# A seven-product mixer kernel: factors and sums of weights issued by ScalarE, stores held back, the last batch's loads begun earlier

## The chip, the cores and the metric

The kernel runs on one core of one Trainium2 chip. The metric is the device time of one execution in microseconds (us); the median of several runs counts, and lower is better.

## What is computed

Four batches of chunked attention (8 heads, 768 positions, head size 64), each followed by a mixer over positions (rank 32) and one over channels (512 to 2048 to 512).

```python
for c in range(nc):                                  # 24 chunks of 32 queries
    k_full = np.concatenate([mem_k, k[:, :, l_start:r_end]], axis=2)
    v_full = np.concatenate([mem_v, v[:, :, l_start:r_end]], axis=2)
    scores = scale * np.matmul(q_c, k_full.transpose(0, 1, 3, 2))
    a = np.exp(scores - np.max(scores, axis=-1, keepdims=True))
    a = a / (np.sum(a, axis=-1, keepdims=True) + 1e-09)
    out[:, :, c_start:c_end] = np.matmul(a, v_full)
...
h = x.transpose(0, 2, 1) @ U @ V                     # x: the attention, heads side by side
u = x + h.transpose(0, 2, 1)
return u + np.maximum(u @ w_ch1, 0.0) @ w_ch2
```

## The kernel before, in words

A batch has six tiles of 128 positions, `x`, in two blocks of three. The wide layer has 16 slices `f` of 128. One w1 step makes `ph` = W1[f] times u of a block in a bank of `ps_h`; ScalarE writes its Relu rounded (`hh`), VectorE the remainder (`hl`); one w2 step (`w2_step`) is nine matmuls of 512 columns that add hh x w2 high, hh x w2 low and hl x w2 high to three banks. `hh` and `hl` come from the pool `hid`, three buffers of each.

Batches 0 and 1 run this plainly (`both_blocks`, `ffn`). During batch 1, `mix` (GpSimd) and `sums` (VectorE subtracts and adds, ScalarE rounds) make, for each of the eight pairs p of slices, five sums and two copies of weights and store them in DRAM (`s_d`): the factors. Each is 256 KB.

Batches 2 and 3 run `fast`: for each p, `products(p)` does seven products in place of eight (`PRODUCTS`; six matmuls of 384 columns each, in three banks b1, b2, b3) and combines them (`ta`, `tb`) into two hidden slices of block 0, whose `hh`, `hl` are made at once (`hid_`), and two of block 1, which are kept in float (`kept`). `first_block(p)` runs the two w2 steps of block 0, as a rule behind `products(p + 1)`; `second_block` makes hh and hl of eight kept slices and runs their w2 steps, once half way and once at the end. A factor's buffer is single: `fetch_factor` can load the factor of p + 1 only when the product of p that reads it has run. The fold of the next batch (`fold_both`: transposes, sums and roundings for `th`, `tl`) is laid between the w2 steps of a batch's last `second_block`.

The attention of batch b + 1 is a generator whose pieces (turn keys, turn queries, scores, softmax, weights times values, the rank-32 mixer) are called between the steps of batch b: `place(n)` runs n pieces. In `fast`, `fast_border` is called after the third and the seventh product, after each w2 step of `first_block` and after those of the first `second_block`; `PLACES` lists the borders at which a piece stands. Its loads are another generator; `serve(n)` issues n of them.

The order on TensorE (PE) and GpSimd is that of the code, written by hand, and so is that of SyncE's queue (SP), which issues every DMA of these batches. SP works strictly in order: a DMA that has to wait holds all behind it. VectorE and ScalarE are ordered by a scheduler from priorities. Buffers of the pool `tk` (19 slots) serve x, loads of k and q, sums, and more; a slot is free again when its last reader, a store too, has ended.

```python
    def fast_border():
        serve(2)
        place(PLACES.count(passed[0]))
        passed[0] += 1
...
                if p + 1 < NF // 2:
                    fetch_factor(p + 1, n)
                elif not last:
                    fetch_factor(0, n)
```

Of the kernel before, what the change touches and what calls it, by code (L numbers as in the profile page):

```python
# [50 lines left out]
SUMS = (("s1", 0, 0, 1, 1, "add"), ("s2", 1, 0, 1, 1, "add"), ("s5", 0, 0, 0, 1, "add"),  # L51
        ("s6", 1, 0, 0, 0, "subtract"), ("s7", 0, 1, 1, 1, "subtract"))
PRODUCTS = (("s5", 6, 0), ("a22", 2, 1), ("s1", 0, 2), ("a11", 1, 0), ("s2", 5, 1), ("s7", 4, 2), ("s6", 3, 0))
PLACES = [0, 2, 4, 6, 8, 10, 11, 13, 14, 16, 18, 20, 22, 23, 24, 25, 27, 29, 31, 33, 35]


@with_exitstack
def chunk_attn_then_mixer_kernel(
# [1035 lines left out]

    x_d = {(b, t): dram.tile([P, CH], F32, name=f"xd{b}_{t}") for b in range(1, B) for t in range(NT)}

    def put_by(b, t):
        nc.sync.dma_start(out=x_d[b, t], in_=xs.pop((b, t)))

    def recall(b, blk):  # L1100
        for t in range(blk * TB, blk * TB + TB):
# [40 lines left out]
    def add_to_x(b, t, bank, last):  # L1142
        x = xs[(b, t)]
        nc.vector.tensor_tensor(out=x, in0=bank, in1=x, op=ALU.add)
        if last:
            nc.sync.dma_start(out=out[b, t * P:(t + 1) * P, :], in_=xs.pop((b, t)))

    accs = {}

# [43 lines left out]
    def both_blocks(pieces, following):  # L1193

        units = []
        for f in range(SPLIT + LEAD):
            if f < SPLIT:
                units.append((0, f, 0, f == 0, None))
            if f >= LEAD:
                g = f - LEAD  # L1200
                units.append((1, g, 1, g == 0, False if g == SPLIT - 1 else None))
        units += [(0, f, 0, False, True if f == NF - 1 else None) for f in range(SPLIT, NF)]
        units += [(1, f, 0, f == SPLIT, True if f == NF - 1 else None) for f in range(SPLIT, NF)]
        prev = []
        for n, (blk, f, where, begins, ends) in enumerate(units):
            while done[0] < min(2 * NF, 2 * f + 1 + (n > LATE)):
                advance(1)
                more_w()
            if n == 2:
                head.close()  # L1210
            solo = n >= 2 * SPLIT
            if n == 2 * SPLIT:
                paced.close()
            for blk_, m, *_ in units[n:n + AHEAD + 1]:
                if m >= SPLIT and blk_ == 1:
                    get_w1l(m)
            if n + AHEAD >= len(units):
                get_w1l(n + AHEAD - len(units))
            w1l = w1ls[f]
            if f >= SPLIT or blk == 1:  # L1220
                del w1ls[f]
            if n == 2 * SPLIT - SOON:
                place(1)
            serve(RATEL if n < 2 * SPLIT else RATES)
            if n > 2 * SPLIT:
                border()
            if n == 0:
                for c, g3 in rest[:2]:
                    join_uT1(turn_x1(c), c, g3)
            hid_ = w1_step(0, blk, f, w1l)  # L1230
            if n == 0:
                decode(2, 4)
                for c, g3 in rest[2:]:
                    join_uT1(turn_x1(c), c, g3)
                decode(1, 1)
                decode(2, 6)
                decode(1, 6)
                decode(3, 2)
            for _ in range(RATE + (3 < n < 12)):
                advance(1)  # L1240
                more_w()
            if n > 2 * SPLIT:
                border()
            prev.append((blk, f, where, begins, ends) + hid_)
            if solo or n % 2 == 0 or ends:
                while len(prev) > (not ends):
                    while done[0] < 2 * prev[0][1] + 2:
                        advance(1)
                        more_w()
                    if n == len(units) - 1 and len(prev) == 1:  # L1250
                        place(TB)
                    w2_step(0, *prev.pop(0))
        following()
# [32 lines left out]
    def store_sums():  # L1286
        while unstored:
            to, s = unstored.pop(0)
            nc.sync.dma_start(out=to.bitcast(F32), in_=s.bitcast(F32))

    def sums(n):
        store_sums()
        for p, name, fa, ca, fb, cb, op in todo[:n]:
            s = slot([P, NCK, P], F32R, "s")
            hi, lo = s[:, 0:2, :], s[:, 2:4, :]
            a, b_ = (whole[2 * p + f][:, 2 * c:2 * c + 2, :] for f, c in ((fa, ca), (fb, cb)))
            nc.vector.tensor_tensor(out=lo.bitcast(F32), in0=a, in1=b_, op=getattr(ALU, op))
            nc.scalar.copy(out=hi, in_=lo.bitcast(F32))
            nc.vector.tensor_tensor(out=lo, in0=lo.bitcast(F32), in1=hi.bitcast(F32), op=ALU.subtract)
            unstored.append((s_d[p, name], s))  # L1300
        del todo[:n]

    def ffn(b, blk, pieces, following):
        prev = []
        for f in range(NF):
            m = f + AHEAD
            if m < NF:
                get_w1l(m)
            elif following is not None:
                get_w1l(m - NF)  # L1310
            serve(RATEL)
            if f % 2 == 0:
                place(pieces[f])
            w1l = w1ls.pop(f)
            hid_ = w1_step(b, blk, f, w1l)
            if b + 1 == CLASSIC and blk == NBLK - 1 and f == NF - 1:
                open_fast()
                for n in range(len(PRODUCTS)):
                    fetch_factor(0, n)
            sums(3)  # L1320
            if f // 2 in MIX[blk]:
                mix(f, w1l)
            if f == NF - TB:
                recall(b, blk)
            if f % 2 == 1:
                place(pieces[f])
            if blk == NBLK - 1 and f == NEARLY:
                open_turned()
            if f >= NF - TB - blk and following is not None:
                following()  # L1330
            prev.append((f, 0, f == 0, True if f == NF - 1 else None) + hid_)
            if f % 2 == 1:
                while len(prev) > (f < NF - 1):
                    w2_step(b, blk, *prev.pop(0))
# [51 lines left out]
    passed = [0]  # L1386

    def fast_border():
        serve(2)
        place(PLACES.count(passed[0]))  # L1390
        passed[0] += 1

    factors = {}

    def fetch_factor(p, n):
        name = PRODUCTS[n][0]
        if n < WLO:
            s = wlo.tile([P, NCK, P], F32R, name="w1l")
        else:
            s = fast_pools[0].tile([P, NCK, P], F32R, name="s", bufs=len(PRODUCTS) - WLO)  # L1400
        nc.sync.dma_start(out=s.bitcast(F32), in_=s_d[p, name].bitcast(F32))
        factors[p, n] = s

    def split_hidden(src):
# [8 lines left out]
    def seven(b, kept, last):  # L1413
# [5 lines left out]
        def products(p):  # L1419
# [8 lines left out]
            for n, (name, i, at_) in enumerate(PRODUCTS):  # L1428
                s = factors.pop((p, n))
                parts = [(s, c, t, c) for c in range(2) for t in (th, tl)] + [(s, 2 + c, th, c) for c in range(2)]  # L1430
                for m, (w, wc, t, c) in enumerate(parts):
# [1 line left out]
                        out=banks[at_], lhsT=w[:, wc, :], rhs=t[:, i, c, :], start=(n < 3 and m == 0),  # L1433
                        stop=(m + 1 == len(parts)), skip_group_check=True,
                    )
                if p + 1 < NF // 2:
                    fetch_factor(p + 1, n)
                elif not last:
                    fetch_factor(0, n)
                with tc.high_priority(offset=HIGH):  # L1440
                    if n == 0:
                        nc.scalar.copy(out=ta, in_=b1)
                    elif n == 1:
                        nc.vector.tensor_tensor(out=ta, in0=b2, in1=ta, op=ALU.subtract)
                    elif n == 2:
                        nc.vector.tensor_tensor(out=tb, in0=b3, in1=ta, op=ALU.add)
                    elif n == 3:
                        nc.scalar.copy(out=kept[2 * p], in_=b1)
                    elif n == 4:
                        hid_[1] = split_hidden(b2)  # L1450
                        nc.vector.tensor_tensor(out=tb, in0=tb, in1=b2, op=ALU.subtract)
                    elif n == 5:
                        nc.vector.tensor_tensor(out=ta, in0=b3, in1=ta, op=ALU.add)  # L1453
                    else:
                        nc.vector.tensor_tensor(out=kept[2 * p + 1], in0=b1, in1=tb, op=ALU.add)
                        hid_[0] = split_hidden(ta)
                if n in (2, 6):
                    fast_border()
            made[p] = hid_
# [17 lines left out]
    def fast(b, following):  # L1477
        n = NF // 2
        products, first_block, second_block = seven(b, {}, b == B - 1)
        passed[0] = 0  # L1480
        for p in range(n):
            if p == n // 2:
                first_block(p - 1)
            products(p)
            if p not in (0, n // 2):
                first_block(p - 1)
            if p == n // 2 - 1:
                recall(b, 1)
                second_block(list(range(n)), False, fast_border)
        recall(b, 0)  # L1490
        second_block(list(range(n, NF)), True, following)
        first_block(n - 1)

    manual = ExitStack()
    manual.enter_context(tc.manual_schedule(engines=FRONT))
# [83 lines left out]
```

## Time and profile before

| what | us |
|---|---|
| median of 3 runs | 688.99 (683.79 to 690.68) |
| profiled execution, its time | 686.5 |
| profiled execution, its span | 684.4 |
| TensorE busy in the span | 647.9 |
| VectorE busy | 359.4 |
| ScalarE busy | 248.6 |
| batch 2 (`fast`) begins, ends | about 375, 551 |
| batch 3 ends | 684 |

A row of waits names the engine and line that stood, what it stood for, the total, the number of times and the longest. A row of windows gives each engine's busy time in that stretch, then the clock that TensorE was granted (1.00 is 2.4 GHz, 0.50 is 1.2 GHz), the mean busy share of the 16 DMA engines and what they moved. In a timeline, brackets hold the idle time ahead of an instruction and what ended it. PE is TensorE, DVE VectorE, ACT ScalarE, SPq the issuing queue of SyncE. Line numbers (L1401) are those of the kernel before.

### The profile page before, as it was taken

To read this page: it belongs to the slowest core of one execution; us is meant where nothing else is said; L and a number is where in the kernel's file an instruction comes from. 1 tells how busy PE (TensorE), PEld (TensorE's weight loads), DVE (VectorE), ACT (ScalarE), POOL (GpSimd) and SP (SyncE) were. 2 spreads that over 40 slices of the span, in tenths; PEclk is the share of its full clock that TensorE was granted. 3 is DMA by queue.
4 is the path that set the end of the run, shared out by engine and by line. 5 is a ranking of instruction groups with operands and counts; after the bars stand their busy time and mean duration, and the time that the engine had idled before them with its cause. 6 is when DMAs were issued, how large, how long until landed. Compare 5 with 4: busy or idle time off the path is not lost.

```text
span 684.4 us, 15529 instructions
## 1 busy us (share of the span) xinstructions
PE 647.9 (95%) x6246; PEld 561.8 (82%) x6246; DVE 359.4 (53%) x735; ACT 248.6 (36%) x616; POOL 45.8 (7%) x72
## 2 busy tenths in 40 slices
PE   7798999999999999889999779899899999999997
PEld 6577999998879998778898668778788799879975
DVE  5977988676535254684537224255434943323323
ACT  4656776565223334342224222332122611212120
POOL 3700000000002122103000000000000000000000
PEclk9999999999999999999999998999999999999999
DMA  8897672583517959695573755941546175507502
GB/s 206 193 326 257 202 242 68 152 232 90 163 49 230 253 153 278 220 296 181 170 256 132 236 149 127 249 101 52 157 140 189 57 245 172 153 1 206 163 1 92
DMA packets 145760, 116.98 MB, mean 171 GB/s; under 512 B 89882, under 2 KB 109082, under 8 KB 145690
## 3 DMA queue, kind: packets, MB, share of 16 engines
q1 hardware_dynamic: 145594, 115.87, 56.9%
q8 instruction: 49, 0.80, 0.5%
q0 software_dynamic: 96, 0.13, 0.1%
q14 instruction: 21, 0.17, 0.1%
HBM read 85.16 MB, written 29.88 MB: 168 GB/s over the span
## 4 chain that ended last, share of the span: by engine, by line
PE 83%; DMA 6%; SPq 4%; DVE 3%; ACT 2%; issue 1%; POOL 0%; ACTq 0%; DVEq 0%
PE ps_h L1130 18%; PE acc L1179 16%; PE ps_h L1432 12%; PE acc L1184 8%; PE ps_a L1432 5%; PE ps_h L1179 4%; PE ps_a L1179 4%; PE ps_a L582 2%; PE ps_a L1184 2%; DMA kn<-in_k_dram 2%; PE ps_a L759 2%; PE ps_h L1184 2%; PE ps_a L656 2%; DMA vb<-in_v_dram 1%; DMA xd<-x 1%
## 5 line engine op out<-in xcount | busy, mean ns | idle before, releaser
L1179 PE MATMUL acc<-w,hh 128*128 128x512 f32 x438 | 114.5, 396 | 1.0 <-DVE w L367 1.0
L1179 PEld LDWEIGHTS acc<-w,hh 128*128 128x128 f32 x438 | 80.2, 188 | 18.9 <-issue 2.5
L1130 PE MATMUL ps_h<-ul,w1h 128*128 128x384 f32 x252 | 85.2, 342 | 2.9 <-issue 2.9
L1130 PE MATMUL ps_h<-uh,w1h 128*128 128x384 f32 x252 | 87.8, 351 | 0.0
L1137 DVE SCALAR_TENSOR_TENSOR hl<-ps_h,hh 128x384 fp32r<-128x384 f32 x63 | 35.0, 555 | 71.4 <-ACT hh L1136 71.0
L1136 ACT ACTIVATE hh<-ps_h 128x384 fp32r<-128x384 f32 x63 | 30.9, 493 | 105.7 <-PE ps_h L1130 105.6
L1184 PE MATMUL acc<-w,hl 128*128 128x512 f32 x219 | 61.8, 390 | 0.0
L1432 PE MATMUL ps_h<-th,w1l 128*128 128x384 f32 x192 | 58.5, 356 | 0.0
L1130 PE MATMUL ps_h<-uh,w1l 128*128 128x384 f32 x252 | 54.7, 339 | 0.0
L1130 PEld LDWEIGHTS ps_h<-uh,w1h 128*128 128x128 f32 x252 | 48.4, 192 | 5.6 <-issue 3.6
L1130 PEld LDWEIGHTS ps_h<-ul,w1h 128*128 128x128 f32 x252 | 48.3, 192 | 1.5 <-issue 0.5
L1184 PEld LDWEIGHTS acc<-w,hl 128*128 128x128 f32 x219 | 41.1, 188 | 8.8
L1130 PEld LDWEIGHTS ps_h<-uh,w1l 128*128 128x128 f32 x252 | 45.3, 189 | 0.0
L1408 DVE SCALAR_TENSOR_TENSOR hl<-kept,hh 128x384 fp32r<-128x384 f32 x32 | 17.9, 558 | 45.0 <-PE ps_a L1184 39.1
L1432 PEld LDWEIGHTS ps_h<-th,w1l 128*128 128x128 f32 x192 | 36.9, 197 | 1.9 <-DVE part L1453 1.0
L1432 PE MATMUL ps_h<-th,s 128*128 128x384 f32 x128 | 35.7, 339 | 0.0
L1179 PE MATMUL ps_a<-w,hh 128*128 128x512 f32 x118 | 33.5, 396 | 1.8 <-ACT hh L1136 1.8
L1408 DVE SCALAR_TENSOR_TENSOR hl<-ps_a,hh 128x384 fp32r<-128x384 f32 x16 | 8.9, 559 | 48.9 <-ACT hh L1407 48.9
L1407 ACT ACTIVATE hh<-kept 128x384 fp32r<-128x384 f32 x32 | 16.8, 525 | 47.4 <-PE ps_a L1179 41.1
L1432 PE MATMUL ps_h<-tl,w1l 128*128 128x384 f32 x96 | 33.4, 348 | 0.0
L1179 PE MATMUL ps_h<-w,hh 128*128 128x512 f32 x104 | 31.9, 429 | 0.0
L1277 POOL TENSOR_TENSOR wv<-w1h,w1l 128x512 f32<-128x512 f32 x16 | 21.2, 1325 | 125.4 <-DMA w1l<-w1ld 114.1
(274 smaller groups left out, 1150.4 us busy)
## 6 DMA issues: line engine op xcount, KB each, us to landing
w1l<-w1ld SPq DMA_DIRECT2D x39, 256.0 KB
rw<-in_moe_w_ch_dram SPq DMA_DIRECT2D x14, 512.0 KB
out_dram<-x SPq DMA_DIRECT2D x24, 256.0 KB
vb<-in_v_dram SPq DMA_DIRECT2D x56, 98.0 KB
raw<-in_moe_w_ch_dram SPq DMA_DIRECT2D x20, 256.0 KB
qn<-in_q_dram SPq DMA_DIRECT2D x36, 128.0 KB
xd<-x SPq DMA_DIRECT2D x18, 256.0 KB
x<-xd SPq DMA_DIRECT2D x18, 256.0 KB
```

Of the source, the lines that this page charges most:

```text
L582: nc.tensor.transpose(out=psv[:, p, r, :], in_=half[:, r, 2 * p:2 * p + 2, :].rearrange("n h d -> n (h d)"), identity=ident,)
L656: nc.tensor.matmul(out=psv[s][CK * i:CK * i + CK, t, p % 2, p // 2, :], lhsT=qt[p // 2][rows, p % 2, NI * t + i, :], rhs=kall[rows, NB * ( ...
L759: nc.tensor.matmul(out=psv[g][CK * i:CK * i + CK, t, j], lhsT=pt[j % 2][rows, 2 * t + j // 2, CK * i:CK * i + CK], rhs=vt[rows, NI * t + i ...
L1130: nc.tensor.matmul(out=ph[:, :TOK], lhsT=w[:, c, :], rhs=u[c], start=(m == 0), stop=(m + 1 == len(parts)),)
L1136: nc.scalar.activation(out=hh, in_=ph[:, :TOK], func=AF.Relu)
L1137: nc.vector.scalar_tensor_tensor(out=hl, in0=ph[:, :TOK], scalar=0.0, in1=hh.bitcast(F32), op0=ALU.max, op1=ALU.subtract,)
L1179: nc.tensor.matmul(out=acc[tt], lhsT=h[:, sl], rhs=w, start=(begins and m == 0), stop=False,)
L1184: nc.tensor.matmul(out=acc[tt], lhsT=hl[:, sl], rhs=w2h[f], start=False, stop=ends is not None)
L1277: nc.gpsimd.tensor_tensor(out=v, in0=w1h[f].bitcast(F32), in1=w1l.bitcast(F32), op=ALU.add)
L1407: nc.scalar.activation(out=hh, in_=src, func=AF.Relu)
L1408: nc.vector.scalar_tensor_tensor(out=hl, in0=src, scalar=0.0, in1=hh.bitcast(F32), op0=ALU.max, op1=ALU.subtract,)
L1432: nc.tensor.matmul(out=banks[at_], lhsT=w[:, wc, :], rhs=t[:, i, c, :], start=(n < 3 and m == 0), stop=(m + 1 == len(parts)), skip_group_c ...
```

## The change

The factors of p + 1 are fetched on ScalarE's queue, at a few places of a step (the first after product 0, three after product 3, one after 4, two after 6); only the first seven go by SP. Stores of sums go by ScalarE too, each behind the next sum's rounding, where before a step's stores went by SP at the next step. Stores of x for later (`put_by`) and of the output are collected in `held` and issued at the next border (`let_go`). Ahead of the first product of batch 2, one `place(1)` opens the attention of batch 3 and `serve(8)` issues the loads of its first keys and queries; a border then serves four loads and not two, and `PLACES` has its first piece at border 3 (before: the opening at 0 and the first piece at 2). Last, `first_block(n // 2 - 1)` and `first_block(n - 1)` move from behind a `second_block` to ahead of it.

```diff
-PLACES = [0, 2, 4, 6, 8, 10, 11, 13, 14, 16, 18, 20, 22, 23, 24, 25, 27, 29, 31, 33, 35]
+PLACES = [3, 5, 7, 9, 11, 13, 14, 16, 18, 20, 22, 23, 24, 25, 27, 29, 31, 32, 33, 35]
...
+    held = []
+
     def put_by(b, t):
-        nc.sync.dma_start(out=x_d[b, t], in_=xs.pop((b, t)))
+        held.append((x_d[b, t], xs.pop((b, t))))
+
+    def let_go():
+        while held:
+            to, x = held.pop(0)
+            nc.sync.dma_start(out=to, in_=x)
...
         if last:
-            nc.sync.dma_start(out=out[b, t * P:(t + 1) * P, :], in_=xs.pop((b, t)))
+            held.append((out[b, t * P:(t + 1) * P, :], xs.pop((b, t))))
+            if b == B - 1:
+                let_go()
...
     def store_sums():
         while unstored:
             to, s = unstored.pop(0)
-            nc.sync.dma_start(out=to.bitcast(F32), in_=s.bitcast(F32))
+            nc.scalar.dma_start(out=to.bitcast(F32), in_=s.bitcast(F32))
 
     def sums(n):
-        store_sums()
...
             nc.scalar.copy(out=hi, in_=lo.bitcast(F32))
+            store_sums()
...
             m = f + AHEAD
+            if f != 1:
+                let_go()
...
     def fast_border():
-        serve(2)
+        let_go()
+        serve(4)
...
-    def fetch_factor(p, n):
+    def fetch_factor(p, n, eng=nc.scalar):
...
-        nc.sync.dma_start(out=s.bitcast(F32), in_=s_d[p, name].bitcast(F32))
+        eng.dma_start(out=s.bitcast(F32), in_=s_d[p, name].bitcast(F32))
...
-                if p + 1 < NF // 2:
-                    fetch_factor(p + 1, n)
-                elif not last:
-                    fetch_factor(0, n)
...
+                    if p + 1 < NF // 2 or not last:
+                        for m in ((0,), (), (), (1, 2, 3), (4,), (), (5, 6))[n]:
+                            fetch_factor((p + 1) % (NF // 2), m)
...
         passed[0] = 0
+        if b + 1 < B:
+            place(1)
+            serve(8)
         for p in range(n):
-            if p == n // 2:
-                first_block(p - 1)
             products(p)
-            if p not in (0, n // 2):
+            if p % (n // 2):
                 first_block(p - 1)
             if p == n // 2 - 1:
+                first_block(p)
                 recall(b, 1)
                 second_block(list(range(n)), False, fast_border)
         recall(b, 0)
+        first_block(n - 1)
         second_block(list(range(n, NF)), True, following)
-        first_block(n - 1)
```

SP's queue near the start of batch 2, before: w1l and s are factors (sd1s_159 is one of p = 1, sd2... of p = 2), kn are keys of batch 3.

```order
L1401 DMA s<-sd1s_159 128x512
L488 DMA kn<-in_k_dram 120x4x64
L491 DMA kn<-in_k_dram 8x4x64
L488 DMA kn<-in_k_dram 120x4x64
L1401 DMA w1l<-sd2s_160 128x512
L1401 DMA w1l<-sd2a_161 128x512
L1401 DMA w1l<-sd2s_162 128x512
L491 DMA kn<-in_k_dram 8x4x64
L488 DMA kn<-in_k_dram 120x4x64
```

The same queue with the change, from the end of the first keys on; qn are queries, out_dram the output of batch 1, vb values.

```order
L488 DMA kn<-in_k_dram 120x4x64
L491 DMA kn<-in_k_dram 8x4x64
L488 DMA qn<-in_q_dram 128x4x64 x4
L1105 DMA out_dram<-x 128x512 x3
L509 DMA mv<-in_mem_v_dram 8x4x64 x2
L488 DMA kn<-in_k_dram 128x4x64 x4
L488 DMA qn<-in_q_dram 128x4x64 x4
L545 DMA vb_102<-mv 8x8x256 x2
```

The factors have left the queue, and the loads of keys, queries and values follow one another; the three stores stand behind the first twelve loads.

ScalarE at step p = 0 of batch 2, before: part is `ta`, the eviction after product 0; kept follows product 3, hh<-ps_a product 4, hh<-part product 5.

```order
L1442 COPY part_5222<-ps_h 128x384
L1448 COPY kept<-ps_h 128x384
L1407 ACTIVATE hh<-ps_a 128x384
L1407 ACTIVATE hh<-part_5222 128x384
L1442 COPY part_5222<-ps_h 128x384
```

The same step with the change.

```order
L1451 COPY part_5222<-ps_h 128x384
L1414 DMA w1l<-sd1s_153 128x512
L1414 DMA w1l<-sd1a_154 128x512
L1414 DMA w1l<-sd1s_155 128x512
L1457 COPY kept<-ps_h 128x384
L1414 DMA w1l<-sd1a_156 128x512
L1420 ACTIVATE hh<-ps_a 128x384
L1414 DMA s<-sd1s_157 128x512
L1414 DMA s<-sd1s_158 128x512
L1414 DMA s<-sd1s_159 128x512
L1420 ACTIVATE hh<-part_5222 128x384
```

Seven issues stand among four operations; the scheduler has put the fetches after products 1 and 2 ahead of the copy that follows product 3.

TensorE near the end of batch 3, before: acc banks belong to `first_block`, ps_h and ps_a here to `second_block`; the end of `first_block(6)` and the first step behind it.

```order
L1184 MATMUL acc_7240<-w_1989,hl 128x512
L1184 MATMUL acc_7241<-w_1989,hl 128x512
L1184 MATMUL acc_7242<-w_1989,hl 128x512
L1179 MATMUL ps_h<-w_1672,hh 128x512 x4
L1179 MATMUL ps_a<-w_1672,hh 128x512 x2
L1184 MATMUL ps_h<-w_1672,hl 128x512 x2
L1184 MATMUL ps_a<-w_1672,hl 128x512
```

The same place with the change.

```order
L1193 MATMUL acc_7242<-w_1989,hl 128x512
L1188 MATMUL acc_7240<-w2last,hh 128x512 x2
L1188 MATMUL acc_7241<-w2last,hh 128x512 x2
L1188 MATMUL acc_7242<-w2last,hh 128x512 x2
L1193 MATMUL acc_7240<-w2last,hl 128x512
L1193 MATMUL acc_7241<-w2last,hl 128x512
L1193 MATMUL acc_7242<-w2last,hl 128x512
L1180 MATMUL acc_7240<-w2last,hh 128x512 x2
L1180 MATMUL acc_7240<-w2last,hl 128x512
```

The two steps of `first_block(7)` (the second, at L1180, goes tile by tile) now follow those of `first_block(6)`, and `second_block` comes behind them as the last work of the kernel.

## Rows read from the trace of the kernel before

**Rows 1.** Page, part 1: busy time, share of the span, instructions.

```profile
PE 647.9 (95%) x6246; PEld 561.8 (82%) x6246; DVE 359.4 (53%) x735; ACT 248.6 (36%) x616; POOL 45.8 (7%) x72
```

**Rows 2.** Waits of PE from 200 us on: total us, times, longest.

```profile
PE ps_a L582 <- DMA kn<-in_k_dram: 9.3, 6, 3.5
PE ps_a L759 <- DMA vb<-in_v_dram: 3.3, 1, 3.3
PE ps_h L1130 <- issue: 2.9, 1, 2.9
PE ps_a L582 <- DMA qn<-in_q_dram: 2.0, 2, 1.7
```

**Rows 3.** Windows of 5 us: busy time by engine, PEclk, DMA share, GB/s.

```profile
380.00:385.00 5.00, 5.00 (x29) 4.67 (x28) 2.68 (x6) 1.50 (x3) 0.00 (x0) 1.00 0.90 262
...
390.00:395.00 5.00, 4.65 (x20) 4.28 (x21) 0.00 (x0) 2.77 (x11) 0.00 (x0) 0.66 0.13 30
...
410.00:415.00 5.00, 3.04 (x11) 2.85 (x12) 0.00 (x0) 1.17 (x5) 0.00 (x0) 0.62 0.42 105
415.00:420.00 5.00, 5.00 (x22) 4.91 (x21) 1.88 (x4) 0.97 (x2) 0.00 (x0) 0.70 0.50 112
...
440.00:445.00 5.00, 4.53 (x15) 3.38 (x16) 0.00 (x0) 2.46 (x11) 0.00 (x0) 0.69 1.02 282
...
485.00:490.00 5.00, 4.33 (x89) 4.16 (x90) 1.42 (x4) 0.48 (x1) 0.00 (x0) 0.66 0.02 4
```

**Rows 4.** Waits of SP's own queue from 200 us on.

```profile
SPq L1401 <- PE ps_h L1432: 136.5, 71, 25.9
```

**Rows 5.** Timeline of SP in batch 2: start us, us, line, DMA.

```profile
388.77 0.40 SPq L488 DMA_DIRECT2D qn<-in_q_dram  x1
393.91 0.34 SPq L1401 DMA_DIRECT2D w1l<-sd2a  x1
395.12 2.44 SPq L1401 DMA_DIRECT2D s<-sd2s  x3
397.61 1.80 SPq L488 DMA_DIRECT2D qn<-in_q_dram  x3
```

**Rows 6.** Timeline of PE, the query transposes that wait for those loads.

```profile
401.07 0.83 PE L582 MATMUL ps_a<-ident,qn 128*128 128x128 f32 x4 [1.71 <-DMA qn<-in_q_dram]
```

**Rows 7.** Chain that ended last, 652 us to the end: start us, us.

```profile
651.84 2.10 PE ps_h L1432 x12
653.94 1.40 PE acc L1179 x6
...
658.07 1.13 PE ps_h L1179 x4
...
676.55 1.36 PE acc L1179 x6
```

**Rows 8.** Timeline in the last `second_block`: ScalarE and VectorE.

```profile
661.96 0.53 ACT L1407 ACTIVATE hh<-kept 128x384 fp32r<-128x384 f32 x1 [1.74 <-PE ps_a L1179]
...
662.71 0.56 DVE L1408 SCALAR_TENSOR_TENSOR hl<-kept,hh 128x384 fp32r<-128x384 f32 x1 [1.69 <-PE ps_a L1184]
```

**Rows 9.** DMA issues of the whole run: count and size of each.

```profile
out_dram<-x SPq DMA_DIRECT2D x24, 256.0 KB
...
kn<-in_k_dram SPq DMA_DIRECT2D x24, 128.0 KB
```

**Rows 10.** Timeline of SP in batch 1, one issue in a full stretch.

```profile
278.13 1.38 SPq L422 DMA_DIRECT2D w1l<-w1ld  x1
```

**Rows 11.** Chain in batch 2's last `second_block`, with one group of fold transposes.

```profile
527.01 1.13 PE ps_h L1179 x4
...
534.54 0.87 PE ps_a L1355 x8
...
547.59 1.36 PE acc L1179 x6
```

**Rows 12.** Window of the second half of batch 1.

```profile
284.00:374.00 90.00, 87.08 (x803) 76.41 (x803) 51.69 (x120) 27.80 (x63) 7.10 (x9) 0.98 0.64 209
```

More of the change, by code (lines that the diff above doesn't have):

```diff
@@ L1318, in ffn @@
                 for n in range(len(PRODUCTS)):
-                    fetch_factor(0, n)
+                    fetch_factor(0, n, nc.sync)
             sums(3)
@@ L1388, in fast_border @@
     def fast_border():
-        serve(2)
+        let_go()
+        serve(4)
         place(PLACES.count(passed[0]))
@@ L1435, in products @@
                     )
-                if p + 1 < NF // 2:
-                    fetch_factor(p + 1, n)
-                elif not last:
-                    fetch_factor(0, n)
                 with tc.high_priority(offset=HIGH):
```

## The prediction

> **What bounds the kernel now.** I read the busy times first: TensorE (PE) is busy 647.9 us of the 684.4 us span [rows 1], so whatever is to be gained is what PE waits for, or does slowly. I then listed PE's waits from 200 us on [rows 2]. The reader sees 14.6 us there that end on a landing transfer: 9.3 us on key loads (kn, six waits), 2.0 on query loads (qn) and 3.3 on one value load (vb). All are loads for the attention of batch 3, which runs beneath batch 2. The other large row, 2.9 us, is "issue": the profile shows no releaser, and I leave it alone.
>
> Next come windows of 5 us around these waits [rows 3]. Behind each long wait the granted clock has fallen: 0.66, 0.62, 0.70, 0.69 and 0.66 of full speed, a mixture of 2.4 GHz and 1.2 GHz, where PE had stood still just before. The lost work is (1 - clock) times PE's busy time in the window: 0.34 x 4.65 + 0.38 x 3.04 + 0.30 x 5.00 + 0.31 x 4.53 + 0.34 x 4.33 = 7.1 us. So the late loads cost 14.6 + 7.1 = 21.7 us.
>
> Why are they late? SP's own waits say it [rows 4]: at line 1401, the fetch of a factor, SP stood 136.5 us for PE's products to release the buffer, 71 times. SP issues in order, so an attention load written behind such a fetch waits with it. In SP's timeline [rows 5] the first query load goes at 388.77, then the queue stands until the factor of 393.91, the three of 395.12 follow, and only then go the other three query loads, at 397.61; PE waits for them at 401.07 [rows 6].
>
> A second loss shows only in the chain of waits. Two w2 steps of `first_block` take 658.07 - 653.94 = 4.13 us, 2.07 each; the eight of `second_block` behind them take 676.55 - 658.07 = 18.48 us, 2.31 each [rows 7]. There ScalarE's `hh<-kept` waits for PE's previous step to have read hh, and VectorE's `hl` for it to have read hl [rows 8]. `hid` has three buffers of each, and in the old order two are held by the pair of `first_block(n - 1)`, which is to run behind; with one left, every step has to wait for the last.
>
> **The change part by part.**
>
> *Factors to ScalarE, loads begun early.* In the new SP order the twelve loads of the first keys and queries stand ahead of the batch's stores, and no factor fetch stands between any loads of the batch. SP is then held only by a buffer that is not yet free. Their first reader on PE moves back, from behind the third product of step p = 1 to behind the seventh: four products, and two take 2.10 us [rows 7], so 4.2 us of extra cover. The attention's last pieces stay where they were (33 and 35 end both lists). I take all 21.7 us as saved; the lower bound is 0, if the transfers are late by themselves.
>
> *What the factor fetches cost on ScalarE.* Each is an issue of 0.34 to 0.45 us by SP's rows [rows 5], and one of SP's in a full stretch took 1.38 [rows 10]. A fetch stands behind an eviction of the same or a later product, or at most one product ahead of its turn, so its buffer is free by about the time it is reached. Per step of seven products (7.35 us by [rows 7]) ScalarE has four operations of about 0.5 us [rows 8] and now seven issues: 2.0 + 7 x 0.35 = 4.5 us, which fits. At 0.7 us an issue it would be 6.9 us, and fit barely. I take 0. Where `first_block` (4.13 us) lies between two steps there is more room still.
>
> *Stores of sums to ScalarE.* Forty stores, 14 to 28 us of issue at 0.34 to 0.7 us, in the batch-1 stage, where from 284 to 374 us ScalarE is busy 27.8 of 90 us [rows 12]. They hide as long as a Relu (`hh`) held up by them stays under the two w-steps (about 4 us) that PE has before it wants it. I take 0, with 10 us as the upper bound.
>
> *Stores put off (`held`).* Six to twelve stores of 256 KB [rows 9] leave together at a border. The first border falls on the two places where seven products follow seven without a `first_block` between, p = 0 to p = 1. In batch 3 that is 12 x 0.26 + 7 x 0.26 = 5.0 MB; at the 262 to 282 GB/s of the busiest windows [rows 3] 18 to 19 us. If both queues get half, the factors (1.84 MB) need 13 to 14 us from about 1.5 us into the step, while the last is wanted at 13.6 us: late by 1 to 2 us, and clock behind it. In batch 2 three stores and eight loads of 128 KB do the same on a smaller scale. Not seen before; I take 2 us for each place, 4 us in all, with 0 and 9 as bounds.
>
> The Trainium skill (DMA: Bandwidth & Descriptors, section "Issuing engines are not separate DMA queues") states that DMAs started by different engines run on the same 16 DMA engines and interleave, so that several issuers save only issue time. It speaks against the change; by it alone the load term would be nothing. The trace shows 136.5 us of waiting in the issuing queue itself, and that is what I weigh more; the rival "transfers" below is what is left of it.
>
> *`first_block(n - 1)` ahead of `second_block`.* The diff's few words don't mention it, but the order shows it in both halves of batches 2 and 3. All three `hid` pairs then serve `second_block`. In batch 3 each of its two halves gains 18.48 - 8 x 2.07 = 1.9 us, so 3.8. In batch 2's second half, 547.59 - 527.01 = 20.58 us [rows 11], less three groups of fold transposes at 0.87 us, leaves 17.97, a gain of 1.4. In its first half attention pieces fill some of the steps: between 0 and 1.9, I take 1.0. Sum 6.2 us. The products that now follow `second_block` at once need its first bank back; that one's addition runs while PE is on the two tiles behind it, so 0.
>
> **The sum.** 686.5 us is the profiled execution's own time (span 684.4). 686.5 - 21.7 - 6.2 + 4.0 = 662.6 us. The median shown, 688.99, lies 2.5 above the profiled execution; for half of that I forecast **664 us**.
>
> **The rivals.**
>
> *ScalarE held.* The forty stores wait on ScalarE for VectorE's last subtraction, and Relus stand behind them. For it: forty issues that ScalarE didn't have, each ending a wait for VectorE. Against it: ScalarE's idle share in [rows 12], and PE's slack before a Relu. Price, by the upper bound above, 8 to 12 us: about 674.
>
> *Transfers.* The loads leave early but land as late, since DMA engines were busy 0.90 in 380 to 385 us and 1.02 in 440 to 445 [rows 3]. Against it: in 390 to 395, amid the waits, the share is 0.13: the engines stood idle while SP stood. If half of the 21.7 stays, 675; if nearly all, about 684, which can't be told from before.
>
> *No gain from the order of blocks.* If banks and not `hid` set the 2.31 us, the 6.2 us stay: 670. Against it: both waits in [rows 8] name the reader of hh and hl.
>
> *Slower: a factor late at every step.* If a fetch on ScalarE reaches its queue so late that its product waits, it happens in each of 14 steps. It decides from (689 - 664) / 14 = 1.8 us a step; at 3 us and 1 us of slow clock behind it, 14 x 4 = 56 us, so 720. For it: one buffer per factor, so nothing is fetched ahead. Against it: from SP the same fetch, begun at most 0.9 us earlier, cost PE no wait that [rows 2] shows.
>
> **How the numbers follow.** Forecast 0.55, ScalarE held 0.14, transfers 0.14, no gain from the order 0.10, slower 0.07. About 1% (7 us) is what a measurement of this kernel can tell from no change. The forecast's own range is 657 to 670, from its 0 to 9 us of new waits and the runs' own spread; the rivals above it reach 675. I give 655 to 677, which leaves out the slower rival, the late end of the transfers and a little more. Faster by over 1% (under 682): all but the slower rival and half of the transfers, 0.86; within 1%: 0.07; slower: 0.07.
>
> **What would show it.** No kn, qn or vb row of more than 1 us in PE's waits between products, and granted clock 1.00 in the windows of batch 2. SP's wait for products gone from its list. `second_block` in 16.5 us where nothing lies between. New waits of PE, if any, on a factor (w1l or s) in step p = 1 of batches 2 and 3. Wrong would be: waits of PE on ScalarE's `hh` in batch 1 (ScalarE held), the same kn waits with loads issued long before (transfers), or factor waits at every step.

## The result and the profile after

The changed kernel takes 664.93 us in the median of four runs (660.79 to 667.49), against 687.58 us for the kernel before in the same series (683.79 to 690.68): a ratio of 0.967, with a 95% interval of 0.959 to 0.974. A second series gave 666.30 us (664.07 to 671.71) against 686.66, ratio 0.972 (0.968 to 0.975). The profiled execution took 667.49 us, of which 665.3 are the span.

Busy time by engine, from the page, answers to [rows 1]:

```profile
PE 635.9 (96%) x6244; PEld 559.2 (84%) x6246; DVE 359.1 (54%) x735; ACT 247.9 (37%) x616; POOL 46.4 (7%) x72
```

TensorE (PE) is busy 12.0 us less for the same work, and idle 29.4 us of the span, where it was 36.5. Its waits from 200 us on (total us, times, longest) answer to [rows 2]:

```profile
PE ps_a L1120 <- DVE ul L1123: 3.4, 1, 3.4
PE ps_h L1137 <- issue: 2.6, 1, 2.6
PE ps_a L759 <- issue: 2.6, 1, 2.6
PE ps_h L1445 <- DVE part L1455: 1.2, 1, 1.2
...
PE ps_h L1445 <- ACT kept L1457: 0.9, 1, 0.9
PE ps_h L1445 <- DMA w1l<-sd1s: 0.6, 1, 0.6
PE ps_h L1445 <- DVE part L1462: 0.3, 1, 0.3
PE ps_h L1445 <- ACT part L1451: 0.3, 1, 0.3
```

Lines have moved (the product, L1432 before, is L1445; the fetch of a factor, L1401, is L1414). No kn, qn or vb row is left. At the top stands a wait that the kernel before does not have, for `ul` in batch 1. Of SP's own waits, those of L1401 for products are gone; what SP stands for most is a store of rows that are not ready (before, at L1146, 68.7 us):

```profile
SPq L1105 <- DVE x L1151: 95.2, 17, 27.3
```

Windows of 5 us at the places of [rows 3] (busy time by engine, granted clock, DMA share, GB/s):

```profile
390.00:395.00 5.00, 4.66 (x24) 4.10 (x24) 1.67 (x3) 0.94 (x2) 0.00 (x0) 1.00 1.02 297
...
410.00:415.00 5.00, 5.00 (x28) 4.29 (x27) 1.95 (x4) 1.05 (x4) 0.00 (x0) 1.00 1.15 297
...
440.00:445.00 5.00, 5.00 (x90) 3.90 (x77) 2.11 (x6) 1.05 (x2) 0.61 (x2) 1.00 0.46 105
```

The granted clock is 1.00 where it was 0.62 to 0.70, and in 390 to 395 us the DMA engines, idle before (0.13), are full. In the chain that ended last, a step of the last `second_block` answers to [rows 7]:

```profile
645.29 0.91 PE ps_h L1188 x4
646.20 0.45 PE ps_a L1188 x2
646.65 0.45 PE ps_h L1193 x2
647.11 0.23 PE ps_a L1193
647.34 0.91 PE ps_h L1188 x4
```

It takes 647.34 - 645.29 = 2.05 us; seven take 659.58 - 645.29 = 14.29 us, 2.04 each, where they took 2.31.

Every run is divided in the same way: batches 2 and 3 begin with the first start of one of their products (`th` as input), and batch 3 ends with the span. The stages are of the one profiled run. Medians are of all runs; ratios leave out one slow execution, 689.36 us with one more hidden pair. Each ratio is to the kernel before in the same series, whose medians lie between 685.61 and 687.58 us, and is not the quotient of the two medians.

| kernel | median us | ratio to before (95%) | batch 2 begins | batch 2 | batch 3 and end |
|---|---|---|---|---|---|
| before | 687.58 | | 374.9 | 176.6 | 132.9 |
| after | 664.93 | 0.967 (0.959 to 0.974) | 379.9 | 156.1 | 129.3 |
| after, second series | 666.30 | 0.972 (0.968 to 0.975) | 377.5 | 155.6 | 128.8 |
| order of blocks alone | 680.09 | 0.991 (0.988 to 0.994) | 376.5 | 178.3 | 128.5 |
| one more hidden pair | 682.40 | 0.994 (0.991 to 0.997) | 377.5 | 172.5 | 129.2 |
| queue alone | 662.94 | 0.967 (0.963 to 0.971) | 372.8 | 154.5 | 133.0 |
| queue and order | 658.14 | 0.959 (0.956 to 0.963) | 374.0 | 152.6 | 129.9 |
| + sums on ScalarE | 663.21 | 0.966 (0.963 to 0.970) | 378.4 | 153.6 | 128.7 |
| + stores put off | 658.90 | 0.961 (0.957 to 0.964) | 374.5 | 153.1 | 129.0 |
| + later places of factors | 658.48 | 0.957 (0.952 to 0.962) | 372.0 | 153.0 | 128.8 |
| after, factors on SyncE | 670.56 | 0.977 (0.973 to 0.981) | 380.1 | 156.3 | 133.1 |
| after, sums on SyncE | 662.00 | 0.964 (0.960 to 0.967) | 372.5 | 153.7 | 130.6 |
| same, stores at once | 665.10 | 0.970 (0.967 to 0.974) | 374.6 | 160.0 | 128.8 |
| same, no early begin | 661.66 | 0.965 (0.960 to 0.969) | 371.6 | 153.1 | 129.2 |

So the change loses 5.0 us up to batch 2, and wins 20.5 in batch 2 and 3.6 in batch 3.

### The profile page after: what moved, and what is told of

The parts are those of the page before. It is cut to its first block, busy times and chain, and to the rows that moved or that the text cites. A ratio compares the mean times of both kernels' runs of the same rounds, so it can differ in the third digit from the quotient of the medians.

```text
span 665.3 us, 15470 instructions
## 1 busy us (share of the span) xinstructions
PE 635.9 (96%) x6244; PEld 559.2 (84%) x6246; DVE 359.1 (54%) x735; ACT 247.9 (37%) x616; POOL 46.4 (7%) x72
## 4 chain that ended last, share of the span: by engine, by line
PE 87%; DVE 4%; DMA 3%; ACT 2%; issue 2%; SPq 1%; POOL 0%; ACTq 0%; DVEq 0%
PE ps_h L1137 19%; PE acc L1188 17%; PE ps_h L1445 12%; PE acc L1193 9%; PE ps_a L1445 4%; PE ps_a L1188 4%; PE ps_h L1188 4%; PE ps_a L582 2%; PE ps_a L759 2%; PE ps_a L1193 2%; PE ps_a L656 2%; PE ps_h L1193 2%; PE ps_a L741 1%; DMA raw<-in_moe_w_ch_dram 1%; DMA w1l<-sd1s 1%
## 5 line engine op out<-in xcount | busy, mean ns | idle before, releaser
L1188 PE MATMUL acc<-w,hh 128*128 128x512 f32 x438 | 116.3, 401 | 1.0 <-DVE w L367 1.0
L1445 PE MATMUL ps_h<-th,w1l 128*128 128x384 f32 x192 | 55.9, 343 | 1.2 <-DMA w1l<-sd1s 0.6
L1445 PEld LDWEIGHTS ps_h<-th,w1l 128*128 128x128 f32 x192 | 35.2, 188 | 4.5 <-issue 1.7
L1445 PE MATMUL ps_h<-th,s 128*128 128x384 f32 x128 | 35.7, 338 | 2.1 <-DVE part L1455 1.2
L1445 PE MATMUL ps_h<-tl,w1l 128*128 128x384 f32 x96 | 32.3, 336 | 0.0
L1188 PE MATMUL ps_h<-w,hh 128*128 128x512 f32 x104 | 28.4, 395 | 0.0
```

Of the source, the lines that this page charges most:

```text
L1188: nc.tensor.matmul(out=acc[tt], lhsT=h[:, sl], rhs=w, start=(begins and m == 0), stop=False,)
L1445: nc.tensor.matmul(out=banks[at_], lhsT=w[:, wc, :], rhs=t[:, i, c, :], start=(n < 3 and m == 0), stop=(m + 1 == len(parts)), skip_group_c ...
```

## The experiments

**The queue alone.** The kernel before; only the engine that issues the factors differs.

```diff
-                    fetch_factor(0, n)
+                    fetch_factor(0, n, nc.sync)
...
-    def fetch_factor(p, n):
+    def fetch_factor(p, n, eng=nc.scalar):
...
-        nc.sync.dma_start(out=s.bitcast(F32), in_=s_d[p, name].bitcast(F32))
+        eng.dma_start(out=s.bitcast(F32), in_=s_d[p, name].bitcast(F32))
```

> The kernel before with one part alone: the factors are issued by ScalarE, at the places of before; no early begin, the stores are not put off, the order of the blocks is the old one. Theory of the queue: SyncE no longer waits for slots, the loads of the last batch come in time, and 14 to 22 us go: 666 to 673 us. Rival (the transfers are the bound, or the last batch begins too late whatever queue it has): under 5 us, 683 to 688 us. Rival (ScalarE is held by the factors' slots): slower than before, with copies of the products late.

24.2 us less than before (662.94 against 687.16 in its series), more than the 14 to 22 expected; in the traces batch 2 is 22.1 us shorter and nothing else moved by more than 2.1. PE's waits from 200 us on:

```profile
PE ps_h L1130 <- issue: 2.6, 1, 2.6
PE ps_a L582 <- DMA kn<-in_k_dram: 2.2, 1, 2.2
PE ps_a L1113 <- ACT qt L642: 0.9, 1, 0.9
```

One kn wait of 2.2 us is left of 14.6 us of waits for loads, and the granted clock from 375 to 527 us is 1.00. Another issuer for one kind of fetch gives as much as the whole change.

**The changed kernel with the factors back on SyncE.**

```diff
-    def fetch_factor(p, n, eng=nc.scalar):
+    def fetch_factor(p, n, eng=nc.sync):
```

> The kernel after with the factors of the products issued by SyncE again, everything else as changed (the early begin of the last batch's loads, the later places, the order of the blocks). Theory of the queue: SyncE waits in its order for a factor's slot, and the loads of the last batch stand behind it, so most of the 21.7 us come back: 678 to 686 us, with TensorE waits for kn, vb or qn in batch 2 again. Rival (the early begin is what brings the loads in time): no change from the kernel after, 663 to 667 us, no such waits. Between the two the early begin would be worth part of it.

670.56 us, between the two, and not as either theory had it. SP stands for factor buffers nearly as long as before (121.3 us at L1414 for products, 51 times), yet PE waits for no kn, qn or vb, and batch 2 takes 156.3 us, as in the changed kernel. So without the other queue the rest of the change brings the loads in time. That it is the early begin is likely, but not shown by itself: the put-off stores, four loads at a border and the later places are in this kernel too. PE now waits for a factor:

```profile
PE ps_a L1445 <- DMA w1l<-sd1a: 5.3, 2, 2.7
```

One of the two waits, 2.6 us, falls in batch 2 (at 391.62), where the changed kernel has 2.7 us of other waits of its products; the other, 2.7 us, in batch 3 (at 547.92), where the changed kernel has 0.5. So the loss against it stands in batch 3 (133.1 us against 129.3). SP's timeline there (start us, us, line, DMA) shows why: nine put-off stores go ahead of the next factor.

```profile
537.67 0.33 SPq L1414 DMA_DIRECT2D w1l<-sd1s  x1
538.05 3.24 SPq L1105 DMA_DIRECT2D xd<-x  x6
541.39 2.38 SPq L1105 DMA_DIRECT2D out_dram<-x  x3
543.86 0.38 SPq L1414 DMA_DIRECT2D w1l<-sd1a  x1
```

**The order of the blocks alone.** The kernel before, with `first_block(n - 1)` ahead.

```diff
         recall(b, 0)
+        first_block(n - 1)
         second_block(list(range(n, NF)), True, following)
-        first_block(n - 1)
```

> The kernel before with one part of the change alone: the last two halves of the first token block stand ahead of the second block's products, in the middle and at the end of each of the last two batches; all loads stay on SyncE. Theory of the sum: six microseconds less than before (1.9 us in each half of batch 3, 1.4 and 1.0 in the halves of batch 2), about 681 to 682 us, a ratio of 0.991; a step of the last second block falls from 2.31 to about 2.05 us. Rival (the banks, not the hidden pairs, set the pace of those steps): no change, 686 to 688 us, steps of 2.3 us as before.

7.1 us less; the interval makes it 4.0 to 8.5. In the one profile, that of the longest of its nine runs (685.3 us), the gain stands in batch 3 alone, 4.4 us; the 2.4 us expected of batch 2 do not show. The steps take 2.04 us:

```profile
663.28 0.91 PE ps_h L1179 x4
...
665.32 0.91 PE ps_h L1179 x4
```

**One more hidden pair, old order.** This separates the hidden pairs from the banks and the order as such.

```diff
-NSLOT = 19
+NSLOT = 18
...
+        if more:
+            hh, hl = (fast_pools[0].tile([P, TOK], F32R, name=name, bufs=1) for name in ("hh2", "hl2"))
...
-                hid_ = split_hidden(kept.pop(f))
+                hid_ = split_hidden(kept.pop(f), f % 2 == 0)
```

> The kernel before with one more pair of hidden tiles for the second block's steps of the last two batches, used by every other step (one slot of the 19 for token rows and weights goes for its room); the order of the blocks is the old one. Theory (a step waits for the one hidden pair that is free): the steps of the last second block take 2.04 us in place of 2.31 us as with the new order, and 4 to 7 us go, 680 to 684 us. Rival (the order itself, by the banks that the first block holds, sets the pace): the steps stay at 2.3 us, 686 to 689 us. The slot less may cost up to some us elsewhere, which does not show in the steps.

682.40 us, and the steps of the last `second_block` take 2.08 us in the old order:

```profile
656.83 0.92 PE ps_h L1179 x4
...
658.90 0.93 PE ps_h L1179 x4
```

A second free pair brings nearly all of the step's gain (2.31 before, 2.04 with the new order), so it was the hidden pairs; what else the order does is not needed to explain it. The whole kernel gains only 3.2 us in its series (685.61 before); what the slot less costs is not separated.

**Queue and order, nothing else.**

> The kernel before with two parts of the change and nothing else: factors issued by ScalarE at the places of before, and the new order of the blocks. Theory that the parts add: the queue alone gave 24 us and the order alone 7 us, so 655 to 658 us, and the rest of the change (stores put off, early begin, later places, sums stored by ScalarE) costs 7 to 9 us together. Rival (the gains overlap, since both parts shorten the same waits of batch 2): 660 to 663 us, and the rest of the change costs 2 to 5 us.

658.14 us, all six runs within 656.16 and 658.34. The two parts add within the noise: their ratios, 0.967 and 0.991, make 0.958 together, and 0.959 is measured. The order gives 4.8 us on top of the queue, and this kernel beats the changed one by 7 to 8 us. The rest of the change costs that much; the next runs ask which part of it.

**Sums stored by ScalarE.** First added to queue and order, then taken from the changed kernel.

```diff
-            nc.sync.dma_start(out=to.bitcast(F32), in_=s.bitcast(F32))
+            nc.scalar.dma_start(out=to.bitcast(F32), in_=s.bitcast(F32))
...
-        store_sums()
...
             nc.scalar.copy(out=hi, in_=lo.bitcast(F32))
+            store_sums()
```

> The kernel with the queue and the order of the blocks alone (658.1 us), and on top the stores of the forty sums issued by ScalarE, right behind the copy of the next sum. Theory that ScalarE is held there: a wait for ul of some 3.4 us at about 286 us, granted clock under 0.9 behind it, batch 2 five to seven us later, 661 to 665 us. Rival (the stores cost nothing, as the sum took them): 656 to 659 us, batch 2 begins at 372 to 375 us.

> The kernel after with the stores of the forty sums of weights issued by SyncE again, at their old place ahead of the next sums. Theory of the sum: the stores on ScalarE cost nothing, so no change, 663 to 667 us. Rival (ScalarE is held by a store that waits for VectorE, as the wait of 3.4 us at 286 us and the granted clock of 0.74 to 0.94 up to 320 us in the kernel after suggest): 3 to 6 us less, 659 to 662 us, and batch 2 begins at about 375 us in place of 380 us.

Added, they cost 5.1 us (663.21 against 658.14); taken away, they give back 2.9 to 4.3 (662.00 against 664.93 and 666.30). In the four profiles with these stores on ScalarE batch 2 begins at 377.5 to 380.1 us, in the nine others with all 19 slots at 371.6 to 376.5. The timeline with queue and order alone, at the attention piece in batch 1 (brackets: idle time ahead, and what ended it):

```profile
281.56 2.34 DVE L1299 TENSOR_TENSOR s<-s 128x256 fp32r<-128x256 f32 x3
281.72 0.50 ACT L1136 ACTIVATE hh<-ps_h 128x384 fp32r<-128x384 f32 x1
282.10 1.24 ACT L642 COPY qt<-ps_a 128x256 f32<-128x256 f32 x4
...
282.82 0.66 PE L1113 MATMUL ps_a<-ident,x 128*128 128x128 f32 x4 [0.91 <-ACT qt L642]
```

and with the stores of sums on ScalarE on top:

```profile
281.56 2.34 DVE L1299 TENSOR_TENSOR s<-s 128x256 fp32r<-128x256 f32 x3
282.20 0.33 ACTq L1289 DMA_DIRECT2D sd6s<-s  x1
282.57 0.49 ACT L1136 ACTIVATE hh<-ps_h 128x384 fp32r<-128x384 f32 x1 [0.75 <-DVE s L1299]
283.60 1.46 ACTq L1289 DMA_DIRECT2D sd6s<-s  x3
...
285.10 0.95 ACT L642 COPY qt<-ps_a 128x256 f32<-128x256 f32 x3 [2.04 <-DVE s L1299]
...
285.36 1.12 PE L1113 MATMUL ps_a<-ident,x 128*128 128x128 f32 x4 [3.42 <-DVE ul L1116]
```

VectorE does the same at the same time in both. On ScalarE the stores wait for its subtractions, and the copies of `qt` behind them begin at 285.10 in place of 282.10; PE's transposes, which need a free bank of `ps_a`, begin 2.5 us later. Without these stores on ScalarE the transposes take the bank that the first copies of `qt` have emptied. With them they take another one, released by `ul`: they begin at 285.36, when no copy of `qt` has ended yet, as the copies' durations show (ns: shortest, median, longest; then first and last start).

```profile
L642 ACT COPY qt<-ps_a x4: 390/402/412, 285.1 to 285.9; 128x256 f32<-128x256 f32 x4
```

So the wait is for `ul`, as the profile has it. `ul` starts at 284.63 in both traces and kept nobody waiting in the first, because the bank of `qt` was free at 282.8; now that one is still full when `ul` ends. Why the program takes the other bank, the trace does not show. That the stores bring it about the runs do show: all four profiles with these stores on ScalarE have the wait of 3.4 us for `ul`, and all ten others have one of 0.9 us for `qt` in its place.

Windows of 280 to 320 us (busy time by engine, granted clock, DMA share, GB/s), of the two kernels in this order:

```profile
280.00:320.00 40.00, 36.72 (x547) 32.68 (x547) 25.83 (x60) 13.48 (x34) 6.44 (x5) 0.96 0.78 248
```

```profile
280.00:320.00 40.00, 33.67 (x406) 29.91 (x405) 23.34 (x56) 12.90 (x32) 5.64 (x4) 0.91 0.65 213
```

With these stores PE loses 40 - 33.67 = 6.3 us standing and 0.09 x 33.67 = 3.0 to the clock, 9.4 together; without them 3.3 and 0.04 x 36.72 = 1.5, 4.8 together. That is 4.6 more, and batch 2 begins 4.4 us later. A second series of the changed kernel asks whether this belongs to the kernel or to one execution:

> The changed kernel itself, beside the two that follow. Theory of the sum: 664 us (655 to 677); a second profile shows whether the 3.4 us wait at 286 us and the slow clock behind it belong to the kernel (they are there again, and the first product of batch 2 begins at about 380 us) or to one execution (375 us or less).

The wait of 3.4 us for `ul` is there again, so it belongs to the kernel. Batch 2 begins at 377.5, half way between 374.9 and 379.9: of the 5.0 us that the first profile lost up to there, half is found again.

**Stores put off.** Added to queue and order (the `held` lines of the change), then taken from the changed kernel with sums on SyncE.

> The kernel with the queue and the order of the blocks alone (658.1 us), and on top the stores of the token rows put off to the next border; no early begin, places of before. Theory of the sum (2 us of new waits at the first steps of batches 2 and 3 each): 661 to 663 us. Rival (they find room among the transfers): 656 to 659 us, and no wait of batch 3's products over 0.5 us. Rival (putting them off frees SyncE): 655 us or less.

> The kernel after with the sums stored by SyncE again (662.0 us) and, on top, every store of the token rows issued at once, as before; the early begin stays. Theory of the sum (put-off stores share the transfers with the first factors of a batch, at 1 to 2 us a batch): 658 to 660 us, the first steps of batch 3 without waits. Rival (putting them off costs nothing): 661 to 663 us. Rival (it is of use, since a store that waits for its rows holds SyncE): 664 us and more, with loads of the last batch late.

Alone they cost 0.8 us, not to be told from nothing, and PE's only wait of batch 3's products over 0.2 us is one of 0.3. With the early begin they are of use: without them 665.10 us, 3.1 more, and batch 2 takes 160.0 us in place of 153.7. SP's timeline without them shows the first key load behind the output stores of batch 1,

```profile
375.05 1.52 SPq L1153 DMA_DIRECT2D out_dram<-x  x3
376.67 0.43 SPq L488 DMA_DIRECT2D kn<-in_k_dram  x1
```

and with them (the changed kernel with sums on SyncE) ahead of these:

```profile
368.40 0.44 SPq L488 DMA_DIRECT2D kn<-in_k_dram  x1
```

The first value loads go at 396.90 without them and at 388.92 with them. PE stands for no load itself: its waits of 1.8 and 1.3 us at key transposes end on VectorE and ScalarE. The chain that ended last leads from the first of them back to a factor fetch on ScalarE (ACTq is its issuing queue) that goes only when a value load has landed:

```profile
399.31 5.16 DMA vb<-in_v_dram
...
404.49 0.33 ACTq L1412
...
404.86 0.50 ACT hh L1418
...
405.39 0.56 DVE hl L1419
405.94 0.47 DVE part L1458
...
406.46 0.67 PE ps_a L582 x4
```

**Early begin and later places.** One run takes the early begin from the changed kernel with sums on SyncE (its edit is below), the other adds only the later places of the fetches to queue and order.

```diff
-PLACES = [3, 5, 7, 9, 11, 13, 14, 16, 18, 20, 22, 23, 24, 25, 27, 29, 31, 32, 33, 35]
+PLACES = [0, 2, 4, 6, 8, 10, 11, 13, 14, 16, 18, 20, 22, 23, 24, 25, 27, 29, 31, 33, 35]
...
-        serve(4)
+        serve(2)
...
-        if b + 1 < B:
-            place(1)
-            serve(8)
```

> The kernel after with the sums stored by SyncE again (662.0 us) and, on top, without the early begin of the last batch: no piece and no loads ahead of the first product of batch 2, two loads at a border in place of four, the places of before. The stores stay put off. Theory (the early begin crowds the transfers of the first steps of batch 2, where factors and results of the attention came 0.6 to 1.2 us late): 656 to 659 us, without the waits of batch 2's products. Rival (the stores put off make those waits): 661 to 663 us, the waits stay. Rival (the early begin is of use even with the factors on ScalarE): 665 us and more, with waits for kn or vb.

> The kernel with the queue and the order of the blocks alone (658.1 us), and on top the factors fetched where the changed kernel fetches them, behind the copies of their step and some of them two or three products later, in place of right behind each product; stores at once, no early begin. Theory that the later places cost nothing, since a factor has a whole step of some 16 us to come: 657 to 660 us, and then the 4 us by which the changed kernel with sums on SyncE (662.0 us) stands above 658.1 us are the early begin's. Rival (the later places crowd the factors together and some come late): 661 to 663 us, with waits of batch 2's or batch 3's products for a factor, and the early begin costs nothing.

The later places cost nothing (658.48 against 658.14). Without the early begin the median is 661.66, as with it (662.00), but its six runs lie between 655.66 and 664.63, and the two kernels nearest to it, with only put-off stores or only later places, took 658.90 and 658.48. No gain of the early begin shows once ScalarE fetches the factors; whether it costs 0 or up to 4 us is not settled. The traces show one small piece of a cost: a wait at an attention piece of batch 2 (L759, "issue") is 1.8 to 2.6 us in the five profiles with the early begin, and at most 0.9 in the others.

## Why the prediction was right, step by step

The time, 664, was met, but in part by luck: two terms were wrong with opposite sign, the put-off stores 3.2 us too dear and the stores of sums 5.1 us too cheap.

- *Late loads, 21.7 us.* Right in cause and size: the queue alone took 22.1 us out of batch 2 and no more than 2.2 us of load waits are left; the clock there went to 1.00. I credited the queue and the early begin together; the queue alone suffices for batch 2, and so does the rest of the change without it, and they don't add. The transfers rival is out: with the same transfers and only another issuer the time is gone. The rule of the Trainium skill cited above (DMA: Bandwidth & Descriptors, "Issuing engines are not separate DMA queues") would have forecast no gain, and failed: SyncE's queue had stood 136.5 us for buffers, and a second issuer takes the loads out of that standing, not only out of the issue time. Whether the two queues run on the same DMA engines, no run here shows.
- *Factor fetches on ScalarE, 0.* Right with the queue alone: batches 2 and 3 have no wait of PE for a factor or for a copy behind a fetch, so the rival of a factor late at every step is out. In the changed kernel it is not quite right. I asked only whether the factor's buffer is free; but in batch 2 ScalarE also stood among the fetches until another transfer had landed, and a copy stood behind:

```profile
391.15 0.33 ACTq L1414 DMA_DIRECT2D w1l<-sd2a  x1
394.99 0.33 ACTq L1414 DMA_DIRECT2D w1l<-sd2s  x1
395.36 0.48 ACT L1457 COPY kept<-ps_h 128x384 f32<-128x384 f32 x1 [3.80 <-DMA w1l<-sd2a]
```

PE waited 0.9 us for this copy and 0.6 for a factor; the chain to its third wait in batch 2, 1.2 us, also passes a fetch on ScalarE.
- *Order of the blocks, 6.2 us.* Right: 7.1 alone, 4.8 on top of the queue. By the traces of that pair batch 2 gains 1.9 (forecast 2.4) and batch 3 3.1 (3.8). The cause, the hidden pairs, is shown by the run with one more of them, so the rival that gave the banks the blame is out.
- *Stores put off, 4.0 us.* Mis-sized: 0.8 measured without the early begin, and with it they save 3.1. I had 5.0 MB move at 262 to 282 GB/s, the busiest windows of before. In the changed kernel the place looks so:

```profile
540.00:545.00 5.00, 4.71 (x27) 4.39 (x27) 1.95 (x4) 0.97 (x2) 0.00 (x0) 1.00 1.02 388
545.00:550.00 5.00, 4.74 (x28) 4.42 (x27) 1.67 (x3) 1.64 (x4) 0.00 (x0) 1.00 1.05 380
```

At 384 GB/s the same 5.0 MB take 13 us, and the last factor is wanted at 13.6. The two waits there, 0.29 and 0.26 us, are for VectorE and ScalarE to empty a bank; the late factor that I priced did not come. In batch 2 the waits of its products, 0.6 to 1.2 us each, come to 2.7 in the changed kernel, but with the put-off stores alone there are none, so these aren't theirs alone; two of the three are those behind the fetches on ScalarE.
- *Stores of sums, 0 us.* The step that failed: 5.1 measured. I set ScalarE's idle time in all [rows 12] against 14 to 28 us of issue, and asked only whether a Relu could be late by 4 us. The Relu was late by 0.85 us (282.57 against 281.72) and hurt nobody. Behind it in ScalarE's order stood the copies of `qt`, 3.0 us late, so that no bank was free for PE's transposes before `ul` had ended, and they stood 3.4 us in place of 0.9: a place without slack that an average over 90 us hides. The rival "ScalarE held" had stores that wait on ScalarE for VectorE, at 8 to 12 us, and was given 0.14. It came true at half its price and by another victim, copies in place of Relus (PE waits for no `hh` there), beside the forecast and not in place of it.

With the measured terms, 686.5 - 22.1 - 5.0 + 5.1 + 0.8 = 665.3 us, against 664.9 and 666.3. Some of this agreement is luck too: the sum takes the put-off stores at their price without the early begin, and the early begin and the later places at nothing. The changed kernel with sums on SyncE stands 3.9 us above queue and order alone (662.00 against 658.14), and the runs of single parts account for 1.1 of them (0.8 for the put-off stores, 0.3 for the later places); the rest is open.

## What to carry to other kernels

A queue that stands for a free buffer delays every load written behind it: give such fetches an issuer on which nothing urgent stands behind them, and stop there. Before moving a store to a compute engine, look at what follows it on that engine at its tightest place, not at the engine's idle share. Two cures for one delay don't add, so do the cheapest alone first: queue and order alone beat the full change by 7 to 8 us.

## What the hardware showed

Transfers moved faster than any window I had read: 388 GB/s at a DMA share of 1.02, against 282 at 1.02 [rows 3], so the share does not tell how many bytes move. A DMA on ScalarE's queue held more than itself: where stores there waited for VectorE, copies began 3.0 us late, and where fetches waited for another transfer to land, ScalarE stood 3.80 us ahead of a copy.
